# Three gather buffers, spaced weight transfers and another order of places in a mixture-of-experts kernel

## The chip, the cores and the metric

The kernel runs on one core of a Trainium2 chip. The metric is device time in microseconds of one execution: a median of 314.38 us over three runs (313.55 to 315.83). Engines are named as the profile names them: PE multiplies matrices (PEld is its weight load), DVE and ACT work elementwise, POOL does iotas, small elementwise work and the indirect transfers, SP issues the plain transfers. Sixteen DMA engines serve all transfers.

## The reference, cut to what matters

Attention with a causal window of 128 positions and four sink positions is computed for 4 batches of 8 heads, 768 positions and 64 columns. Its rows, 3072 of 512 columns, go into a mixture of 8 experts with a capacity of 80 rows each:

```
logits = x @ w_gate;  expert_idx = argmax(logits);  gate_w = softmax(logits)[expert_idx]
for e in range(8):
    tok_idx = rows with expert_idx == e, the 80 with the largest gate_w if there are more
    h = maximum(x[tok_idx] @ w1[e], 0)
    out[tok_idx] = gate_w[tok_idx] * (h @ w2[e])      # all other rows of out stay 0
```

w1[e] is 512 x 1024 and w2[e] 1024 x 512, both float32: 2 MB each, 33.5 MB for all experts.

## The kernel before, in words

The program has three stages. The attention (up to about 195 us of the profile) works in ticks and writes its rows to the scratch tensor x_rows. The ranking (to about 212 us) finds for each expert the row numbers of its 80 tokens, in idx_in. The experts' stage follows, and the change lies there.

**Experts.** For each expert e, an indirect transfer on POOL gathers its 80 rows into xg_e (line 1210). `tokens(e)` turns them on PE into px (line 1245), which DVE copies to xs. `ffn1(e)` is 128 matmuls with w1 into ph (line 1259), `ffn2(e)` 128 matmuls with w2 into py (line 1274), `rows(e)` turns the result back (pry, line 1290) and scatters it to the output by an indirect transfer on POOL (line 1302). PE's order is written out by hand: ffn1(0), tokens(1), ffn1(1), tokens(2), ffn2(0), ffn1(2), tokens(3), rows(0), ffn2(1), and so on; the last blocks are ffn1(7), rows(5), ffn2(6), ffn2(7) with rows(6) in its middle, rows(7). So there are 16 blocks of 128 matmuls.

**Weights.** A weight matrix comes as two halves of 1 MB, each by four transfers of 256 KB from SP (`load_weight`, lines 288 to 303). The 32 halves are numbered n = 0 to 31 in the order of use; block number j of PE uses n = 2j and 2j + 1. There are 17 places in SBUF (NA + NB + NC = 6 + 7 + 4). Ten halves are issued during the attention and the ranking (n = 0 to 9). Seven more, n = 10 to 16, are issued in the loop of lines 1209 to 1214, where with `hold=True` POOL first writes one element of the place (line 298): the transfer has to wait for that write, and the write stands on POOL behind the gather of the same turn. Half n = 17 + k takes the place of an earlier half, which `in_home` chooses, and waits until PE has read that half for the last time. Before, this is the half number 1 + 7k // 4 (through `in_home`, for a place used twice, the first user's place).

**What sets the order on SP.** Every transfer of SP signals one of eight semaphores, in turn, and waits first until the transfer eight places before it, on the same semaphore, has landed. So at most eight transfers of SP are under way. Up to the weight n = 16 the order of SP is written out (`manual_schedule`); behind that the planner of the library places the transfers where it finds them ready.

Of the kernel before, what the change touches and what calls it, by code (L numbers as in the profile page):

```python
# [8 lines left out]
F32 = mybir.dt.float32  # L9
# [11 lines left out]
E, F = 8, 1024  # L21
DM = H * D
# [5 lines left out]
SINK, WIN, CAP = 4, 128, 80  # L28
# [215 lines left out]
def attention_moe(ctx: ExitStack, tc, q, k, v, n_sink, window, w_gate, w1, w2, capacity, q_t, k_t, v_t, vs_t, wg_t, out):  # L244
    nc = tc.nc
# [37 lines left out]
    wsrc = [(which, e, half) for which, e in order for half in range(2)]  # L283
    wtiles = {}
    homes = [(wpool, n) for n in range(NA)]
    in_home = []

    def load_weight(hold=False):
        n = len(wtiles)
        which, e, half = wsrc[n]  # L290
        src = (w1, w2)[which][e].rearrange("(g c p) f -> g p c f", g=2, p=P)[half]

        k = n - NA - NB - NC
        in_home.append(n if k < 0 else in_home[1 + 7 * k // 4])
        pool, m = homes[in_home[n]]
        t = pool.tile([P, 2 * F], F32, tag=f"w{m}", name=f"w_{which}_{e}_{half}", bufs=1)
        if hold:
            po.memset(t[0:1, 0:1], 0.0)
        to = t.rearrange("p (c f) -> p c f", c=src.shape[1])
        for i in range(0, 2 * F, DM):  # L300
            c, f = divmod(i, src.shape[2])
            nc.sync.dma_start(to[:, c, f:f + DM], src[:, c, f:f + DM])
        wtiles[(which, e, half)] = t

    zeros = const.tile([P, DM], F32, name="zeros")
# [2 lines left out]
    with ExitStack() as actx:  # L308
        wk = actx.enter_context(tc.tile_pool(name="wk", bufs=2))
        sm = actx.enter_context(tc.tile_pool(name="sm", bufs=2))  # L310
# [17 lines left out]
        NG = B * NPB  # L328
# [598 lines left out]
        for n in range(NA):  # L927
            at(W0 + WD * n, load_weight)
# [67 lines left out]
        with tc.manual_schedule():  # L996
            n = 0
# [87 lines left out]
            for _ in range(2):  # L1085
                load_weight()
# [3 lines left out]
            rows_keep_scaled(g0, 1, "xr")  # L1090
            rows_write(g0, 1, nc.sync)
            load_weight()
            gate_logits(i, 1)
            keys_turn(i - 1, 1)
# [68 lines left out]
    with ExitStack() as fctx:  # L1163
# [2 lines left out]
        wk = fctx.enter_context(tc.tile_pool(name="fw", bufs=2))  # L1166
        sm = fctx.enter_context(tc.tile_pool(name="fsm", bufs=1))
        xg = {}
        for e in range(E):
            xg[e] = sm.tile([CAP, DM], F32, name=f"xg_{e}")  # L1170
        chain = ExitStack()
        chain.enter_context(tc.manual_schedule(engines={ve.engine, po.engine}))
        with ExitStack() as sctx:
# [28 lines left out]
        with ExitStack() as wctx:  # L1202
            wps = wctx.enter_context(tc.tile_pool(name="ps_warm", bufs=1, space=PSUM))
            wt = wps.tile([P, 512], F32, name="warm1")
            for _ in range(20):
                pe.matmul(wt[0:CAP, 0:480], hot[:, NNEW - 1], hot[:, 0:6].rearrange("p t c -> p (t c)"), start=True, stop=True)
        line = ExitStack()
        line.enter_context(tc.manual_schedule(engines={nc.sync.engine}))
        for e in range(E):
            po.indirect_dma_start(out=xg[e], out_offset=None, in_=x_rows,  # L1210
                                  in_offset=bass.IndirectOffsetOnAxis(ap=idx_in[:, e:e + 1], axis=0),
                                  bounds_check=NT - 1, oob_is_err=False)
            if e > 0:
                load_weight(hold=True)
        while len(wtiles) < NA + NB + NC:
            load_weight(hold=True)
        line.close()
        gsel = sm.tile([CAP, E], F32, name="gsel")
        po.tensor_tensor(gsel, tab[:, 0], tab[:, 1], ALU.add)
# [22 lines left out]
        def tokens(e):  # L1242
            px = ps_xs.tile([P, DC, CAP], F32, tag="px", name=f"px_{e}")
            for c in range(DC):
                pe.transpose(px[:, c], xg[e][:, c * P:(c + 1) * P], ident[0:CAP, 0:CAP])  # L1245
            xts[e] = wk.tile([P, DC, CAP], F32, tag="xs", name=f"xs_{e}")
            ve.tensor_copy(xts[e], px)  # L1247

        def ffn1(e):
            need(0, e)  # L1250
            x = xts.pop(e)
            h = wk.tile([P, HC, CAP], F32, tag="h", name=f"h_{e}")
            for half in range(2):
                ph = ps_h.tile([P, HC // 2, CAP], F32, tag="ph", name=f"ph_{e}_{half}")
                for f in range(HC // 2):
                    fc = half * (HC // 2) + f
                    for c in range(DC):
                        for m in range(2):
                            pe.matmul(ph[m * D:(m + 1) * D, f], columns(0, e, c, fc * P + m * D),  # L1259
                                      x[:, c], start=(c == 0), stop=(c == DC - 1), skip_group_check=True)  # L1260
                ac.activation(h[:, half * (HC // 2):(half + 1) * (HC // 2)], ph, AF.Relu)  # L1261
            hs[e] = h
# [41 lines left out]

        chain.enter_context(tc.manual_schedule(engines={pe.engine, ac.engine}))
        tokens(0)
        for e in range(E):
            ffn1(e)
            if e + 1 < E:
                need(0, e + 1)  # L1310
                tokens(e + 1)
            if e > 1:
                rows(e - 2)
            if e > 0:
                ffn2(e - 1)
# [66 lines left out]
```

## Time and profile before

| | |
|---|---|
| median of three runs | 314.38 us (313.55 to 315.83) |
| the profiled execution, its own time | 318.28 us |
| its span, first to last instruction | 316.5 us |
| mean granted TensorE clock in it | 0.969 |
| PE busy (matmuls) | 285.1 us, 90% |
| weight transfers of 256 KB | 128, median 5.5 us from issue to landing |

Of the 316.5 us, PE is busy nearly throughout, so the profile is read by stage. From 218.1 us, where ffn1(0) begins, to 310 us PE works on the experts; the windows view gives the share of the 16 DMA engines and the transferred GB/s of each stretch, the chain of waits gives the order of PE's work and the idle time between.

### The profile page before, as it was taken

To read this page: it belongs to the slowest core of one execution; us is meant where nothing else is said; L and a number is where in the kernel's file an instruction comes from. 1 tells how busy PE (TensorE), PEld (TensorE's weight loads), DVE (VectorE), ACT (ScalarE), POOL (GpSimd) and SP (SyncE) were. 2 spreads that over 40 slices of the span, in tenths; PEclk is the share of its full clock that TensorE was granted. 3 is DMA by queue.
4 is the path that set the end of the run, shared out by engine and by line. 5 is a ranking of instruction groups with operands and counts; after the bars stand their busy time and mean duration, and the time that the engine had idled before them with its cause. 6 is when DMAs were issued, how large, how long until landed. Compare 5 with 4: busy or idle time off the path is not lost.

```text
span 316.5 us, 10925 instructions
## 1 busy us (share of the span) xinstructions
PE 285.1 (90%) x4253; PEld 228.3 (72%) x4253; DVE 168.6 (53%) x562; ACT 162.2 (51%) x658; POOL 164.7 (52%) x367
## 2 busy tenths in 40 slices
PE   7498999999998999998999999979878988999991
PEld 2265777877777878785768787647777978989880
DVE  5344887785988788899895969940000000000001
ACT  0656787878777787874678765800111111111210
POOL 4297787848898668885748595558101011011111
PEclk9679999999999999999999999969999999999998
DMA  6999125398851699873135002977999998686601
GB/s 189 338 341 405 44 70 197 132 286 275 282 201 70 227 272 386 352 218 121 42 127 202 34 35 63 304 301 212 278 383 382 372 382 287 207 260 209 248 25 51
DMA packets 32747, 69.71 MB, mean 220 GB/s; under 512 B 4272, under 2 KB 5296, under 8 KB 32304
## 3 DMA queue, kind: packets, MB, share of 16 engines
q1 hardware_dynamic: 31664, 66.31, 61.3%
q0 software_dynamic: 1024, 2.62, 2.9%
q8 instruction: 36, 0.59, 0.8%
q14 instruction: 23, 0.19, 0.2%
HBM read 55.02 MB, written 13.89 MB: 218 GB/s over the span
## 4 chain that ended last, share of the span: by engine, by line
PE 60%; DVE 15%; ACT 9%; issue 7%; POOL 6%; DMA 2%; POOLq 0%; ACTq 0%; DVEq 0%
PE ph L1259 12%; PE sc L510 12%; PE py L1274 12%; PE xp L604 7%; PE pp L563 6%; ACT prob L547 4%; DVE gt L768 3%; ACT pt L575 2%; PE pl L670 2%; DVE gt L765 2%; DVE sc L530 2%; DVE nm L537 2%; PE warm L420 2%; PE pr L637 2%; PE xp L598 1%
## 5 line engine op out<-in xcount | busy, mean ns | idle before, releaser
L547 ACT ACTIVATE prob<-sc,nm 128x132 f32<-128x132 f32 (+1 forms) x192 | 68.9, 377 | 4.6 <-DVE nm L537 4.5
L510 PE MATMUL sc<-k,q 64*128 64x260 f32 (+1 forms) x384 | 58.7, 410 | 8.9 <-ACT prob L547 8.4
L1302 POOL DMA_INDIRECT out_dram<-y,idx x8 | 7.3, 918 | 82.0 <-ACT y L1291 71.9
L575 ACT COPY pt<-pp 128x512 f32<-128x512 f32 x48 | 28.2, 587 | 42.1 <-PE pp L563 34.6
L510 PEld LDWEIGHTS sc<-k,q 64*128 64x128 f32 x384 | 30.8, 190 | 24.4 <-ACT prob L547 15.6
L530 DVE COPY_PREDICATED sc<-upper,sc 128x256 f32<-128x256 int8 x80 | 33.8, 422 | 19.8 <-PE sc L510 11.2
L1259 PE MATMUL ph<-xs,w 128*64 128x80 f32 x1024 | 38.9, 233 | 5.5 <-issue 4.4
L537 DVE TENSOR_REDUCE nm<-sc 128x2 f32<-128x264 f32 (+1 forms) x96 | 41.4, 431 | 3.3
L1247 DVE COPY xs<-px 128x320 f32<-128x320 f32 x8 | 3.9, 492 | 72.7 <-PE px L1245 66.6
L1274 PE MATMUL py<-h,w 128*64 128x80 f32 x1024 | 38.6, 234 | 4.0 <-issue 3.5
L1259 PEld LDWEIGHTS ph<-xs,w 128*64 128x64 f32 x1024 | 37.0, 137 | 6.9 <-issue 5.3
L1274 PEld LDWEIGHTS py<-h,w 128*64 128x64 f32 x1024 | 36.5, 137 | 6.2 <-issue 4.6
L547 ACT ACTIVATION_READ_ACCUMULATOR prob<-sc,nm 128x1 f32 x192 | 40.7, 212 | 0.0
L583 POOL TENSOR_SCALAR_AFFINE_SELECT own<-pt 128x512 f32<-128x512 f32 (+1 forms) x48 | 28.6, 595 | 20.3 <-ACT pt L575 19.6
L604 PE MATMUL xp<-pt,v 128*64 128x128 f32 x384 | 37.4, 288 | 0.0
L563 PEld LDWEIGHTS pp<-ident,prob 128*128 128x128 f32 x192 | 20.8, 144 | 16.5 <-issue 10.5
L563 PE MATMUL pp<-ident,prob 128*128 128x128 f32 x192 | 32.3, 292 | 0.0
L604 PE MATMUL xp<-own,v 128*64 128x128 f32 x320 | 31.1, 273 | 0.0
L590 POOL TENSOR_SCALAR_AFFINE_SELECT pt<-pt 128x512 f32<-128x512 f32 (+1 forms) x48 | 27.8, 578 | 3.3
L1261 ACT ACTIVATE h<-ph 128x320 f32<-128x320 f32 x16 | 7.0, 438 | 43.0 <-PE ph L1259 33.9
L604 PEld LDWEIGHTS xp<-pt,v 128*64 128x64 f32 x384 | 21.4, 137 | 3.5 <-POOL pt L590 0.2
L654 POOL TENSOR_TENSOR xr<-xr,rs 128x512 f32<-128x512 f32 x21 | 22.0, 1049 | 2.9 <-ACT xr L642 2.7
(177 smaller groups left out, 470.7 us busy)
## 6 DMA issues: line engine op xcount, KB each, us to landing
w<-in_moe_w_dram SPq DMA_DIRECT2D x128, 256.0 KB, 5.5
v<-in_v_t_dram SPq DMA_DIRECT2D x12, 512.0 KB, 7.2
out_dram<-zeros SPq DMA_DIRECT2D x24, 256.0 KB, 3.0
x_rows<-xr SPq DMA_DIRECT2D x24, 256.0 KB, 2.5
q<-in_q_t_dram SPq DMA_DIRECT2D x11, 512.0 KB, 7.1
k<-in_k_t_dram SPq DMA_DIRECT2D x3, 1584.0 KB, 8.3
k<-in_k_t_dram SPq DMA_DIRECT2D x1, 1056.0 KB, 9.5
vst_raw<-in_vs_t_dram SPq DMA_DIRECT2D x4, 256.0 KB, 6.8
```

The costliest lines, as they stand in the source:

```text
L510: pe.matmul(sc[:, h, c0:c0 + w], qs[g][r, hp, j % 2 * P:(j % 2 + 1) * P], ks[b][r, hp, k0:k0 + w], start=True, stop=True)
L530: ve.copy_predicated(own, upper, sc[:, :, 0:P])
L537: ve.tensor_reduce(out=nm, in_=sc[:, :, lo_c:hi_c], axis=AX.X, op=ALU.max, negate=True)
L547: ac.activation(prob[:, a, h, p0:], sc[:, h, lo_c:hi_c], AF.Exp, bias=nm[:, h:h + 1], scale=1.0, accum_out=ssum[:, n, 2 * hp + h:2 * hp + ...
L563: pe.transpose(pp[:, a, h], prob[:, a, h, SINK:], ident)
L575: ac.copy(pt, st.pop((t, "pp")))
L583: po.affine_select(out=own[:, a0:], in_=pt[:, a0:], pattern=[[0, 2 - a0], [0, 2], [1, P]], compare_op=ALU.is_ge, fill=0.0, base=0, channel ...
L590: po.affine_select(out=pt[:, a0:], in_=pt[:, a0:], pattern=[[0, 2 - a0], [0, 2], [-1, P]], compare_op=ALU.is_gt, fill=0.0, base=0, channel ...
L604: pe.matmul(xp[h * D:(h + 1) * D, a * P:(a + 1) * P], val[:, (2 * hp + h) * D:(2 * hp + h + 1) * D], pr[:, a, h], start=False, stop=(a == ...
L654: po.tensor_tensor(xr, xr, gst[(i0, "rs")][:, n, :, None].to_broadcast([P, H, D]), ALU.mult)
L1259: pe.matmul(ph[m * D:(m + 1) * D, f], columns(0, e, c, fc * P + m * D), x[:, c], start=(c == 0), stop=(c == DC - 1), skip_group_check=True)
L1274: pe.matmul(to[m * D:(m + 1) * D, dc], columns(1, e, k, dc * P + m * D), h[:, k], start=(k == 0), stop=(k == HC - 1), skip_group_check=True)
```

## The change

It has four parts. (1) Three gather buffers take the place of eight: gathers 0 to 2 are issued at first, gather e + 3 behind `tokens(e)`, into the buffer that `tokens(e)` has read. (2) Of the seven halves n = 10 to 16 only the first two are held by a write of POOL. (3) From n = 10 on, three transfers of one element stand among every five transfers of weights: 88 weight transfers get 52 small ones, from wg_t into the tile `spaced`. (4) Half 17 + k takes the place of half k.

```diff
@@ -284,6 +284,7 @@
     in_home = []
+    spaced = []
 
     def load_weight(hold=False):
@@ -291,7 +292,7 @@
         k = n - NA - NB - NC
-        in_home.append(n if k < 0 else in_home[1 + 7 * k // 4])
+        in_home.append(n if k < 0 else in_home[k])
         pool, m = homes[in_home[n]]
@@ -300,6 +301,11 @@
             c, f = divmod(i, src.shape[2])
             nc.sync.dma_start(to[:, c, f:f + DM], src[:, c, f:f + DM])
+            if spaced:
+                j = spaced[0]
+                if 3 * (j + 1) // 5 > 3 * j // 5:
+                    nc.sync.dma_start(spaced[1][0:1, j:j + 1], wg_t[0:1, 0, 0:1])
+                spaced[0] += 1
         wtiles[(which, e, half)] = t
@@ -1166,8 +1172,8 @@
         xg = {}
-        for e in range(E):
-            xg[e] = sm.tile([CAP, DM], F32, name=f"xg_{e}")
+        NG = 3
+        xgs = [sm.tile([CAP, DM], F32, name=f"xg_{n}") for n in range(NG)]
@@ -1204,16 +1210,22 @@
+        spaced += [0, sm.tile([1, 4 * len(wsrc)], F32, name="spaced")]
         line = ExitStack()
         line.enter_context(tc.manual_schedule(engines={nc.sync.engine}))
-        for e in range(E):
+
+        def gather(e):
+            xg[e] = xgs[e % NG]
             po.indirect_dma_start(out=xg[e], out_offset=None, in_=x_rows,
                                   in_offset=bass.IndirectOffsetOnAxis(ap=idx_in[:, e:e + 1], axis=0),
                                   bounds_check=NT - 1, oob_is_err=False)
+
+        for e in range(NG):
+            gather(e)
             if e > 0:
                 load_weight(hold=True)
         while len(wtiles) < NA + NB + NC:
-            load_weight(hold=True)
+            load_weight()
         line.close()
@@ -1245,6 +1257,8 @@
             ve.tensor_copy(xts[e], px)
+            if e + NG < E:
+                gather(e + NG)
```

**SP, from the last weight of the ranking (n = 9, w_1_1) on.** A name such as w_3_0 gives the expert and the half (the matrix is left out, the last number is the buffer's). Before:

```order
L302 DMA w_1_1_3464<-in_moe_w_dram 128x512 x4
L302 DMA w_3_0_3668<-in_moe_w_dram 128x512 x4
L302 DMA w_3_1_3677<-in_moe_w_dram 128x512 x4
L302 DMA w_2_0_3686<-in_moe_w_dram 128x512 x4
L302 DMA w_2_1_3695<-in_moe_w_dram 128x512 x4
L302 DMA w_4_0_3704<-in_moe_w_dram 128x512 x4
L302 DMA w_4_1_3713<-in_moe_w_dram 128x512 x4
L302 DMA w_3_0_3722<-in_moe_w_dram 128x512 x4
```

The same place now:

```order
L303 DMA w_1_1_3464<-in_moe_w_dram 128x512 x4
L307 DMA spaced<-in_wg_t_dram 1x1 x12
L303 DMA w_3_0_3664<-in_moe_w_dram 128x512 x2
L307 DMA spaced<-in_wg_t_dram 1x1
L303 DMA w_3_0_3664<-in_moe_w_dram 128x512 x2
L307 DMA spaced<-in_wg_t_dram 1x1
L303 DMA w_3_1_3675<-in_moe_w_dram 128x512
L307 DMA spaced<-in_wg_t_dram 1x1
L303 DMA w_3_1_3675<-in_moe_w_dram 128x512 x2
L307 DMA spaced<-in_wg_t_dram 1x1
```

The pattern of two, two and one weight with a small transfer behind each group begins with n = 10, but twelve small transfers stand in front of it.

**SP, behind the part that is written out (from the last transfers of n = 16 on), now:**

```order
L307 DMA spaced<-in_wg_t_dram 1x1
L303 DMA w_3_0_3713<-in_moe_w_dram 128x512
L303 DMA w_3_1_4354<-in_moe_w_dram 128x512 x4
L303 DMA w_5_0_4362<-in_moe_w_dram 128x512 x4
L303 DMA w_5_1_4369<-in_moe_w_dram 128x512 x4
L303 DMA w_4_0_4530<-in_moe_w_dram 128x512 x4
L303 DMA w_4_1_4537<-in_moe_w_dram 128x512 x4
L303 DMA w_6_0_4544<-in_moe_w_dram 128x512
L307 DMA spaced<-in_wg_t_dram 1x1
L303 DMA w_6_0_4544<-in_moe_w_dram 128x512
L307 DMA spaced<-in_wg_t_dram 1x1
```

The twelve small transfers that the code puts among the 20 of n = 17 to 21 are those that the planner has moved to the front: these 20 weight transfers stand without any between them, and from n = 22 on the pattern is back.

**POOL, from its last write of the ranking (parts) on.** Before:

```order
L1140 TENSOR_TENSOR parts<-later,os 128x8
L1210 DMA xg_3589<-x_rows,idx_in 80x512
L1210 DMA xg_3590<-x_rows,idx_in 80x512
L298 MEMSET w_3_0_3668 1x1
L1210 DMA xg_3591<-x_rows,idx_in 80x512
L298 MEMSET w_3_1_3677 1x1
L1210 DMA xg_3592<-x_rows,idx_in 80x512
L298 MEMSET w_2_0_3686 1x1
```

Now:

```order
L1219 DMA xg_3591<-x_rows,idx_in 80x512
L299 MEMSET w_3_1_3675 1x1
L1231 TENSOR_TENSOR gsel<-tab 80x8
L1232 TENSOR_TENSOR gsel<-gsel,tab 80x8
L1219 DMA xg_3589<-x_rows,idx_in 80x512
L1219 DMA xg_3590<-x_rows,idx_in 80x512
L1219 DMA xg_3591<-x_rows,idx_in 80x512
L1219 DMA xg_3589<-x_rows,idx_in 80x512
L1316 DMA out_dram<-y_4052,idx 3072x512
L1219 DMA xg_3590<-x_rows,idx_in 80x512
L1316 DMA out_dram<-y_4208,idx 3072x512
```

Gathers 3 to 6 stand in front of the first scatter and gather 7 between the first two; each waits for PE's px of the buffer's last user.

## Rows read from the trace of the kernel before

**Rows 1.** The page: span and DMA queues (packets, MB, share of 16 engines).

```profile
span 316.5 us, 10925 instructions
...
q1 hardware_dynamic: 31664, 66.31, 61.3%
...
q8 instruction: 36, 0.59, 0.8%
```

**Rows 2.** Who waited for whom from 208 us on: us, times, longest.

```profile
PEld py L1274 <- DMA w<-in_moe_w_dram: 0.7, 1, 0.7
...
PE ph L1259 <- issue: 4.4, 6, 1.0
PE py L1274 <- issue: 3.5, 4, 1.8
```

**Rows 3.** The chain of waits in the experts' stage: start us, us, what.

```profile
231.86 1.76 issue
233.62 3.05 PE py L1274 x82
236.68 0.07 PE ph L1259
...
236.75 1.52 PE ph L1259 x44
238.27 0.73 issue
239.00 3.12 PE ph L1259 x83
...
244.38 0.51 issue
...
267.04 0.55 issue
267.59 4.10 PE py L1274 x113
...
297.64 0.36 PE ph L1259 x4
...
303.72 2.43 PE py L1274 x64
```

**Rows 4.** Windows of 10 us: engines' busy us, then PE clock, DMA share, GB/s.

```profile
230.00:240.00 10.00, 7.51 (x203) 7.13 (x203) 0.49 (x1) 0.60 (x2) 0.00 (x0) 1.00 1.05 385
...
270.00:280.00 10.00, 10.00 (x268) 9.61 (x265) 0.49 (x1) 1.99 (x4) 0.91 (x1) 1.00 0.66 218
```

**Rows 5.** DMA view of the stretch from 236.4 to 236.5 us.

```profile
q8 instruction: 1, 0.02, 68.4%
```

**Rows 6.** DMA view of the stretch from 269.6 to 269.9 us.

```profile
q8 instruction: 1, 0.02, 18.4%
```

**Rows 7.** DMA view of the stretch from 298.8 to 299.1 us.

```profile
q8 instruction: 1, 0.02, 28.4%
```

**Rows 8.** Tile w on SP, from 240 to 258 us (durations in ns: min/median/max).

```profile
L302 SPq DMA_DIRECT2D w<-in_moe_w_dram x26: 327/328/1205, 239.8 to 257.5; - x26
...
DMA to landing us min/median/max: 5.2/5.6/5.9
```

**Rows 9.** Tile w on SP, from 265 to 273.5 us.

```profile
L302 SPq DMA_DIRECT2D w<-in_moe_w_dram x8: 328/430/622, 265.5 to 272.5; - x8
...
DMA to landing us min/median/max: 2.6/3.6/4.9
```

**Rows 10.** SP's own waits, from 214 us on: us, times, longest.

```profile
SPq L302 <- PE ph L1259: 11.2, 4, 4.1
SPq L302 <- PE py L1274: 9.3, 4, 3.6
SPq L302 <- POOL w L298: 6.9, 1, 6.9
```

**Rows 11.** Timeline from 207 to 224 us: start us, us, what.

```profile
208.67 0.21 POOL L1140 TENSOR_TENSOR parts<-later,os 128x8 f32<-128x8 f32 x1
...
214.01 0.96 POOL L1210 DMA_INDIRECT xg<-x_rows,idx_in  x1 [0.31 <-issue]
214.97 0.09 POOL L298 MEMSET w<- 1x1 f32 x1
```

**Rows 12.** Tile xg, whole span.

```profile
DMA to landing us min/median/max: 3.2/8.1/9.2
```

**Rows 13.** Tile ints: a transfer of a few bytes from SP.

```profile
L450 SPq DMA_DIRECT2D ints<-in_window_dram x1: 328/328/328, 10.8 to 10.8; - x1
```

## The prediction

> **What bounds the kernel now.** The change touches only the experts' stage, so I read that stage. First the list of waits: on PE's matmuls of the two blocks the idle time that counts waits for no engine and hardly for a weight (0.7 us once); it is put down to "issue", 4.4 us in 6 pieces and 3.5 us in 4 [rows 2]. That is 7.9 us in ten stalls, and PE is busy through the rest of the stage. Then the chain of waits, for where the stalls stand. Between the one that ends at 233.62 and the next at 238.27 PE does 82 + 1 + 44 = 127 matmuls [rows 3]. The others stand at the same distance, so it is a count of instructions and not a place in the program that makes them. A matmul has a weight load beside it, so 127 pairs are some 255 instructions.
>
> Next the DMA queues: queue 8, named instruction, moves 36 packets of together 0.59 MB, 16.4 KB each [rows 1]. PE's stalls are its own program arriving late, in blocks of some 256 instructions. The views of the single packets give their delay. PE resumes at 233.62 and the next such packet starts between 236.4 and 236.5 [rows 3, 5], 2.8 to 2.9 us later. A packet takes 1.1 us (0.8% of 16 engines times 316.5 us, over 36 [rows 1]), and 1.4 to 1.5 us after its end PE resumes, at 239.00 [rows 3]. I read this as: the next block is asked for when PE enters the one in hand. From asking to use it is then 5.4 us here (239.00 - 233.62), while 127 pairs take 4.65 us (233.62 to 238.27) or, with eight transposes among them, 5.38 us (239.00 to 244.38) [rows 3]. The missing part is the stall.
>
> The delay goes with the number of weights under way. From 240 to 258 us, 26 transfers go out in 17.7 us, one per 0.71 us, each landing after 5.6 us [rows 8]: eight are under way, at 385 GB/s and a DMA share of 1.05 [rows 4]. With four under way [rows 9], PE resumes at 267.59 and the packet starts between 269.6 and 269.9 [rows 3, 6], 2.0 to 2.3 us later. With nearly none, PE resumes at 297.64 and the packet starts between 298.8 and 299.1 [rows 3, 7], 1.2 to 1.5 us later. With 2.55 us for the packet and its arrival, the whole delay is 5.4 us at eight, 4.6 to 4.9 at four, 3.8 to 4.1 at none, against the 4.65 to 5.38 us that a block lasts.
>
> **The change part by part.** *The small transfers* take three of SP's eight semaphores, so that five weights and not eight are under way. The delay with five lies between the row at four and the row at eight: 4.6 to 5.4 us. I take 4.9, nearest to four, which is the mean length of a block: the stalls go, but for 0.5 us in all. The bounds for the eight or so blocks concerned are 0 and 8 times half of 0.55 us [rows 3], 2.2 us.
>
> *Their order* gives some back. Between n = 17 and 21 the 20 weights stand without small ones, so eight are under way again for 20 x 0.71 = 14.2 us. With 28 spaced weights from 215.1 us on, that is about 235 to 249 us, two or three blocks. Stalls under eight are 0.51 to 0.73 us there [rows 3]; I take 2.5 x 0.6 = 1.5 us, bounds 0.5 and 2.2. The twelve small ones in front can go once POOL's last write of the ranking is done, 208.88 us, and the first weight behind them waits anyway for POOL's hold at 214.97 [rows 11], a wait in which SP stood 6.9 us [rows 10]. Twelve issues of 0.33 to 0.43 us [rows 8, 9, 13] and one round of landings fit in; if not, n = 10 comes 1 us late, and PE needs it only in block 5, around 250 us. Cost nothing, under that cover.
>
> *SP's time*: 52 issues more. A small one took 0.33 us [rows 13], weights without a wait 0.43 [rows 9]: five weights with three small ones cost SP at most 8 x 0.43 = 3.44 us, with one long issue of 1.2 us [rows 8] 4.6 us, where five weights need 5 x 0.71 = 3.55 us of DMA. SP can become slower than the DMA engines. What covers that: the last half is wanted by ffn2(7), which starts at 303.72 [rows 3], and the loads end at 215.1 + 88 x 0.71 + 3 = 281 us at the DMA's pace; at SP's worst pace 215.1 + 68/5 x 4.6 + 14.2 + 3 = 295 us. Nothing is late.
>
> *The places*: SP waited 11.2 + 9.3 us for PE to free a place [rows 10], and the DMA share fell to 0.66 there [rows 4]. Half k is free earlier than half 1 + 7k // 4, so these waits go. On PE that is worth nothing, as no weight was late; what it triggers is that the loads crowd into 215 to 281 us. More blocks see a full DMA, none behind it does. Without the spacing that would be more stalls; with it, it is in the 0.5 us above.
>
> *The gathers*: five of 0.96 us on POOL [rows 11] leave the start and follow px. They land after 3.2 to 9.2 us [rows 12], and tokens(e + 3) comes at least two blocks, 10 us, later; this is hidden. On POOL each stands before a scatter that waits for later work of PE anyway. The five holds and five early gathers no longer delay n = 12 to 16, which PE does not wait for. Cost nothing.
>
> **The sum.** 7.9 - 0.5 - 1.5 = 5.9 us off PE's line, which runs on to the last scatter. The profiled execution took 318.28 us (span 316.5) and would take 312.4. The median stands 3.9 us below that execution; the difference is not in these rows, so I take the 5.9 us off the median: 308.5 us. With the bounds, 7.9 - 2.2 - 2.2 = 3.5 to 7.9 - 0.5 = 7.4 us, that is 307.0 to 310.9.
>
> **The rivals.**
>
> *Depth does not matter.* The packet may be late because the engines are busy at all, not because of what is queued. For it: share 1.05 with eight, and I have no row with five. Against it: two packets with busy engines around them, 2.8 us at eight and 2.0 to 2.3 us at four. Then every block from 223 to 281 us stalls, some ten of 0.6 to 0.8 us, about 7 us: 313.5 us, 0.9 less than now. [...]
>
> *Half of it.* Five under way behave nearer to eight, and a stall of some 0.3 us stays at each block: 7.9 - 10 x 0.3 - 1.5 = 3.4 us, 311.0. The spread of the delays at four allows it.
>
> *Slower: five under way do not fill the DMA.* If each weight still needs its 5.6 us [rows 8] with five under way, five take 5.6 us instead of 3.55. The last half is then there at 215.1 + 68/5 x 5.6 + 14.2 + 3 = 308.5 us, where ffn2(7) would start at 303.72 - 5.9 = 297.8: 10.7 us of waiting for 5.9 won, 319.2 us. It decides where the round takes over 5.25 us; at 4.9 the loads are in time but for 1 us. For it: the slowest of the rows at four took 4.9 us [rows 9]. Against it: others there took 2.6, and the 5.6 us are 8 x 0.71, a queue and not a latency.
>
> **How the numbers follow.** The forecast has 0.60, half of it 0.15, depth without effect 0.15, slower 0.10. The predicted time is the forecast's 308.5. The range of 306.5 to 313.7 takes in its bounds, the half and most of the case without effect, and leaves about 0.2 out, mostly on the slow side. A measurement of this kernel tells 1%, 3.1 us, from no change. Faster by over 1% (under 311.2): 0.60 and most of the half, 0.69. Within 1%: the case without effect, the rest of the half and the mild end of the slow case, 0.24. Slower by over 1%: 0.07.
>
> **What would show it.** In the chain of waits after, "issue" pieces on PE between 223 and 300 us should sum to about 2 us and stand mostly between 235 and 255. Landing of weights should be near 3.5 us outside that stretch and 5.6 in it. The last weight should be issued before 285 us and the DMA stand empty after. SP should no longer wait for PE. It would be wrong if "issue" pieces stay at 0.5 us and more with landings of 3.5 us (depth does not matter), or if PE waits for DMA w from about 285 us on (loads too slow).

## The result, and the profile after

Over 20 runs each the changed kernel has a median of 312.88 us (308.21 to 317.28), the kernel before 316.13 us (312.08 to 318.75): ratio 0.9886, interval 0.9854 to 0.9917. The ratio leaves out the executions that lie over 1.5% above their kernel's fastest. By it the change is worth 3.6 us (the two medians differ by 3.25), where 5.9 of 314.38 us (ratio 0.981) were forecast. In a later session the same two gave 0.979 (0.972 to 0.986). The direction held, and so did the cure of the stalls; the wait for late weights, which the sum put at nothing, was several us.

The profiled execution took 313.70 us. First its page and the list of waits from 214 to 300 us (engine, line and tile that waited, what for; us, times, longest), which answer to [rows 1, 2, 10]:

```profile
span 312.0 us, 10964 instructions
...
q1 hardware_dynamic: 31768, 66.31, 63.3%
...
q8 instruction: 36, 0.59, 0.8%
```

```profile
PEld py L1288 <- SPq L1342: 2.7, 3, 2.0
...
PE py L1288 <- SPq L1342: 2.2, 3, 1.8
PE ph L1273 <- issue: 2.0, 2, 1.6
...
PEld py L1288 <- DMA w<-in_moe_w_dram: 0.2, 1, 0.2
```

The instruction packets are as many as before. "Issue" on PE's matmuls fell from 7.9 to 2.0 us and is absent from the blocks of py; a wait that was not there has come, on py, for "SPq L1342". The list of SP's own waits no longer has PE's 20.5 us:

```profile
SPq L303 <- DMA w<-in_moe_w_dram: 26.6, 48, 1.8
...
SPq L303 <- PE ph L1273: 0.3, 1, 0.3
```

The timeline of PE shows where both stand (start us, us, line, tiles, count, in brackets the idle time before it and what ended it). First 249 to 256 us, then the last two blocks:

```profile
249.78 2.31 PE L1288 MATMUL py<-h,w 128*64 128x80 f32 x61
251.86 1.13 PE L1273 MATMUL ph<-xs,w 128*64 128x80 f32 x26
254.58 1.61 PE L1273 MATMUL ph<-xs,w 128*64 128x80 f32 x41 [1.59 <-issue]
```

```profile
289.34 4.96 PE L1288 MATMUL py<-h,w 128*64 128x80 f32 x128
294.88 0.91 PE L1288 MATMUL py<-h,w 128*64 128x80 f32 x20 [0.58 <-ACT yt L1296]
297.61 0.36 PE L1288 MATMUL py<-h,w 128*64 128x80 f32 x4 [1.81 <-SPq L1342]
298.14 0.42 PE L1288 MATMUL py<-h,w 128*64 128x80 f32 x4 [0.17 <-SPq L1342]
298.77 2.67 PE L1288 MATMUL py<-h,w 128*64 128x80 f32 x36 [0.21 <-SPq L1342]
301.37 0.78 PE L1304 MATMUL pry<-ident,yt 128*80 128x128 f32 x4
302.08 2.43 PE L1288 MATMUL py<-h,w 128*64 128x80 f32 x64
```

The 1.59 us stand where eight weights are under way again, n = 17 to 21 (issued from 239.7 to 254.7 us), as the prediction had it. That these are the cause is not shown: the kernel with six in order, below, stalls longest at the same place. The other wait is in the first half of ffn2(7). The releaser's name there, an instruction of SP's queue at the program's end, is a guess of the view. The counts tell more: the first 32 matmuls of this half go through the eight blocks of rows of w2 in turn, four matmuls each, and each of the last four blocks is one transfer of n = 31. PE does 20, then stops, does four, four, and then the rest: it stood before the last three transfers. SP issued the last at 293.50 us. The windows view (busy us of each engine, PE's clock, DMA share, GB/s), to be held against [rows 4]:

```profile
230.00:240.00 10.00, 10.00 (x272) 9.72 (x270) 0.49 (x1) 1.98 (x4) 1.91 (x2) 1.00 0.95 293
270.00:280.00 10.00, 10.00 (x276) 9.72 (x271) 0.49 (x1) 2.12 (x5) 0.91 (x1) 1.00 0.89 300
...
295.00:302.00 7.00, 4.80 (x68) 3.95 (x68) 0.00 (x0) 0.00 (x0) 0.00 (x0) 0.76 0.23 77
```

PE is busy in the whole of both old windows. The DMA engines move 293 and 300 GB/s in these two windows, where before it was 385 and then 218. In the last window the granted clock is 0.76, after PE had stood: 1.00 up to 298 us, 0.50 from 299 to 301 us (over the same window it is 1.00 in the one profile of this kernel without such a wait, the last below). Of ffn2(7)'s first half 36 matmuls took 2.67 us, where 64 take 2.43. So the late weights cost more than the 2.2 us of waiting: this half took 7.20 us (294.88 to 302.08). Before it took 2.92, from the first of these lines to the second:

```profile
303.72 2.43 PE L1274 MATMUL py<-h,w 128*64 128x80 f32 x64 [0.58 <-ACT yt L1282]
...
306.64 2.44 PE L1274 MATMUL py<-h,w 128*64 128x80 f32 x64
```

### The profile page after: what moved, and what is told of

Its sections match the earlier page's. It is cut to its first block, busy times and chain, and to the rows that moved or that the text cites. A ratio compares the mean times of both kernels' runs of the same rounds, so it can differ in the third digit from the quotient of the medians.

```text
span 312.0 us, 10964 instructions
## 1 busy us (share of the span) xinstructions
PE 283.7 (91%) x4253; PEld 228.3 (73%) x4253; DVE 168.3 (54%) x562; ACT 161.9 (52%) x658; POOL 164.4 (53%) x362
## 5 line engine op out<-in xcount | busy, mean ns | idle before, releaser
L516 PE MATMUL sc<-k,q 64*128 64x260 f32 (+1 forms) x384 | 57.9, 405 | 9.1 <-ACT prob L553 8.7
L1288 PE MATMUL py<-h,w 128*64 128x80 f32 x1024 | 39.8, 238 | 2.9 <-SPq L1342 2.2
L1288 PEld LDWEIGHTS py<-h,w 128*64 128x64 f32 x1024 | 37.4, 140 | 5.3 <-SPq L1342 2.7
L1273 PE MATMUL ph<-xs,w 128*64 128x80 f32 x1024 | 37.9, 233 | 3.3 <-issue 2.0
L569 PEld LDWEIGHTS pp<-ident,prob 128*128 128x128 f32 x192 | 20.5, 143 | 16.2 <-issue 10.1
L1219 POOL DMA_INDIRECT xg<-x_rows,idx_in x8 | 8.0, 996 | 31.2 <-PE px L1257 25.9
```

The source lines that it names most:

```text
L516: pe.matmul(sc[:, h, c0:c0 + w], qs[g][r, hp, j % 2 * P:(j % 2 + 1) * P], ks[b][r, hp, k0:k0 + w], start=True, stop=True)
L569: pe.transpose(pp[:, a, h], prob[:, a, h, SINK:], ident)
L1288: pe.matmul(to[m * D:(m + 1) * D, dc], columns(1, e, k, dc * P + m * D), h[:, k], start=(k == 0), stop=(k == HC - 1), skip_group_check=True)
```

## Experiments

Sixteen runs were made, in four sessions on three chips, some of them of a kernel that had run already; each ratio is against the kernel before in the same session. "Stage" is from the first matmul of ffn1(0) to the first of ffn2(7) in the profile, "half" from there to ffn2(7)'s second half, "issue" that of PE's matmuls in the experts' stage, the transposes among them. Each profile is one execution.

| kernel | ratio (95%) | stage, half us | issue us | last weight issued |
|---|---|---|---|---|
| before, three profiles | 1 | 85.6, 85.1, 84.4; 2.9 | 7.9, 6.1, 7.0 | 294.2, 292.4, 292.8 |
| changed, three profiles | 0.9886 (0.985 to 0.992); 0.979 (0.972 to 0.986) | 78.6, 78.8, 77.3; 7.2, 2.9, 6.7 | 2.0, 2.2, 1.6 | 293.5, 292.7, 291.9 |
| no small transfers (8) | 1.008 (1.004 to 1.012) | 83.1; 2.9 | 5.6 | 283.8 |
| seven in order | 0.997 (0.992 to 1.001) | 83.4; 2.9 | 5.5 | 284.7 |
| six in order, twice | 0.989 (0.983 to 0.996); 0.978 (0.972 to 0.985) | 78.8, 80.2; 2.9 | 2.9, 2.6 | 290.2, 288.6 |
| five in order | 1.003 (0.999 to 1.006) | 81.0; 6.5 | 0 | 296.3 |
| five, last 24 free | 0.989 (0.984 to 0.994) | 79.3; 3.6 | 0.2 | 292.5 |
| transfers of 128 KB, none small | 1.121 (1.116 to 1.127) | 121.3; 7.9 | 1.1 | 340.0 |

**How many are under way.** The small transfers were left out, or put in a fixed order on SP (so that the twelve no longer run ahead), in three proportions:

```diff
# no small transfers
-        spaced += [0, sm.tile([1, 4 * len(wsrc)], F32, name="spaced")]
# in order: SP's written order to the end of the stage
-        line = ExitStack()
-        line.enter_context(tc.manual_schedule(engines={nc.sync.engine}))
+        chain.enter_context(tc.manual_schedule(engines={nc.sync.engine}))
...
-        line.close()
# six; seven
-                if 3 * (j + 1) // 5 > 3 * j // 5:
+                if 2 * (j + 1) // 6 > 2 * j // 6:
+                if (j + 1) // 7 > j // 7:
```

> The changed kernel without its small transfers: gathers and places as changed, eight weights under way throughout. Theory A (the queue of weights delays PE's instruction blocks; five under way cure it, and the price is that the loads get slower and the last weights come late): the stalls are back, some ten blocks of 0.6 to 0.7 us, 6 to 7 us in all, and the late weights at the end (4.4 us) are gone: about 2 us above the changed kernel, ratio to the kernel before 0.992 to 1.000, issue pieces of 6 us and more from 218 us on. Theory B (the stalls went for another reason, the order of places or the gathers): few stalls, no late weights, ratio to before about 0.975.

> The changed kernel with SP's order written out to the end, so that the small transfers stand where the program has them: five weights under way throughout, also for the 20 weights that had none between them. Theory A: the stall of 1.6 us of the stretch 241 to 252 us goes, but 20 weights take 0.95 us each instead of 0.7, the last weight comes 4 to 5 us later, and PE waits for it: 4 to 5 us above the changed kernel, ratio to before 1.000 to 1.007, PE's wait inside ffn2(7) 8 to 11 us instead of 4.4. Theory C (the wait at the end comes from the twelve small transfers in front or from a single late transfer, not from the pace of the loads): no later than the changed kernel, ratio 0.98 to 0.99.

> As the kernel in order, but two small transfers per six weights: six under way throughout. Theory A: a weight takes about 0.8 us, the loads end at about 213 + 88 x 0.8 = 284 us and nothing is late; stalls small, 0.2 us in ten blocks: 4 us below the changed kernel, ratio to before 0.973 to 0.982. Theory D (five is needed, six stalls like eight): stalls of 0.5 us and more at most blocks, ratio 0.99 to 1.00.

> As the kernel in order, but one small transfer per seven weights: seven under way. Theory A: a weight takes 0.73 us, nothing is late, stalls of about 0.4 us at ten blocks, 3 to 4 us: ratio to before 0.98 to 0.99, between six and eight under way. Theory D: as with eight, 0.99 to 1.00.

Issue is 5.6, 5.5, 2.9 and 2.6, 0 us for eight, seven, six, five. Theories B and D fall, though seven stalls as eight does, where I had expected 3 to 4 us and a ratio of 0.98 to 0.99. That no block stalls with five in order, while every one has as many instructions as before, shows that the depth of the loads delays PE's program: in the traces of the kernel before and of the changed one each of the twelve stalls ends 2.3 to 3.2 us behind the start of a packet of queue 8, named instruction. The series does not part the bytes that are queued from the rate at which they move: from 260 to 280 us that falls too, 370, 358, 323 and 285 GB/s. Against the rival by which the number queued does not matter as long as the engines are busy stands the DMA share in the same stretch: 1.02 with eight, where issue is 5.6 us, and still 0.89 with five, where it is 0.

Another queue may play a part. The kernel with six in order has its longest stall at 254.83 us, with never more than six weights under way, and the changed kernel has one of 1.56 to 1.59 us there in each of three profiles:

```profile
254.83 2.37 PE L1271 MATMUL ph<-xs,w 128*64 128x80 f32 x63 [1.82 <-issue]
```

From 250 to 256 us a gather and a scatter moved together here, in queue 0. The DMA view of that stretch, for six in order and then for the kernel before, which has none of queue 0:

```profile
q1 hardware_dynamic: 868, 1.58, 78.1%
q0 software_dynamic: 128, 0.33, 15.1%
```

```profile
q1 hardware_dynamic: 1271, 2.31, 103.8%
q8 instruction: 1, 0.02, 1.2%
```

The three profiles of the changed kernel have 127 or 128 of these packets there. But with 121 of them five in order has no stall there, and with 128 the second profile of six in order has one of 0.35 us. So they are a candidate for the long stall, not its shown cause.

The loads pay for the smaller depth. The view of the tile w on SP from 255 to 280 us gives the transfers issued in those 25 us and the time from issue to landing, for eight, seven, six and five under way:

```profile
L303 SPq DMA_DIRECT2D w<-in_moe_w_dram x33: 327/328/1248, 255.0 to 279.4; - x33
...
DMA to landing us min/median/max: 4.9/6.2/7.0
```

```profile
L303 SPq DMA_DIRECT2D w<-in_moe_w_dram x32: 327/328/1227, 255.2 to 279.5; - x32
...
DMA to landing us min/median/max: 4.4/5.1/6.7
```

```profile
L303 SPq DMA_DIRECT2D w<-in_moe_w_dram x30: 327/328/1079, 255.1 to 279.7; - x30
...
DMA to landing us min/median/max: 3.9/4.9/6.5
```

```profile
L303 SPq DMA_DIRECT2D w<-in_moe_w_dram x26: 327/328/1417, 255.6 to 279.2; - x26
...
DMA to landing us min/median/max: 3.1/4.6/6.4
```

From seven to five a transfer lands hardly sooner, 5.1 to 4.6 us, so fewer under way means fewer landed: one per 0.76, 0.78, 0.85 and 0.94 us. Five in order issues its last weight at 296.3 us. PE waits for weights from 278 us on, sooner than expected, and for less inside ffn2(7) (the half takes 6.5 us):

```profile
PE ph L1271 <- DMA w<-in_moe_w_dram: 2.3, 2, 1.4
PE py L1286 <- DMA w<-in_moe_w_dram: 1.6, 3, 0.8
```

Theory A holds, theory C falls. Besides seven, two sizes of mine were off: without small transfers the kernel is slower than expected (1.008, not 0.992 to 1.000), though its one profile, 316.0 us of a median of 318.0, shows no reason; and six gained less than expected in the first of its two comparisons.

**The end alone.** Five in order, with no small transfers among the last 24 weights:

```diff
-            if spaced:
+            if spaced and n < 26:
```

> Five under way, in order, for the first 64 weights from half 10 on, and no small transfers for the last 24. If the late weights of the kernel with five throughout (last issue 296.3 us) were the pace of the loads: 24 weights at 0.7 instead of 0.94 us put the last issue at about 290.5 us, nothing is late, and the price is a stall of 0.5 to 1 us at two or three of the last blocks: below five in order by 1% or more, ratio to before 0.980 to 0.992 by the chip. If the late weights have another cause, as five in order, within 0.5% of the kernel before.

As expected in the time, 1.4% below five in order (across two sessions), and the late weights became fewer but did not go: the last is issued at 292.5 us, not 290.5, and PE waits 2.9 us for weights from 284 us on. The stalls that I expected in the last blocks, with eight under way again, did not come (0.2 us of issue); the waits for weights there may have given PE's program the time, which no run shows.

**Bytes or transfers.** Without small transfers, every weight transfer from n = 10 on cut in two of 64 rows:

```diff
-            nc.sync.dma_start(to[:, c, f:f + DM], src[:, c, f:f + DM])
+            for p in (range(0, P, P // 2) if n >= NA + 4 else (0,)):
+                q = P // 2 if n >= NA + 4 else P
+                nc.sync.dma_start(to[p:p + q, c, f:f + DM], src[p:p + q, c, f:f + DM])
```

> No small transfers; from half 10 on each weight transfer is cut in two of 64 rows, 128 KB: eight are under way as in the kernel without small transfers, but with half the bytes. If the bytes queued ahead of PE's instruction packet make the stalls: issue on PE falls from 5.6 us to 2 us or less, as with four of 256 KB; the loads are slower than with five, 1.0 us or more per 256 KB, and the end waits for them: ratio 1.00 to 1.02. If it is the number of transfers under way: stalls of 5 us and more, as without small transfers.

```profile
PE py L1289 <- DMA w<-in_moe_w_dram: 18.6, 20, 2.1
PE ph L1274 <- DMA w<-in_moe_w_dram: 9.2, 6, 2.1
...
PE py L1289 <- issue: 1.1, 4, 0.4
```

Issue is nearly gone, but this does not tell bytes from transfers, because fewer than eight were under way. SP's own waits from 214 to 340 us show it, here first and then for whole transfers without small ones:

```profile
SPq L305 <- POOL w L299: 6.2, 1, 6.2
SPq L305 <- PE ph L1274: 0.8, 1, 0.8
```

```profile
SPq L303 <- DMA w<-in_moe_w_dram: 27.1, 59, 1.7
```

By this view SP never waited for the transfer eight places before. An issue took 595 ns (median; 328 for a whole transfer), close to the 0.70 us between two issues, so SP set the pace. The loads fell to 202 GB/s from 260 to 280 us, far worse than expected. Whether bytes or transfers count stays open.

**Each part on the kernel before.**

```diff
# small transfers only, in order: the edits on load_weight, spaced and SP's order alone
# places only
-        in_home.append(n if k < 0 else in_home[1 + 7 * k // 4])
+        in_home.append(n if k < 0 else in_home[k])
# gathers only: the edits on xg, gather(e) and the holds alone
# six in order, eight gathers
-        NG = 3
+        NG = 8
```

> The kernel before with three small transfers to five weights (in order, five under way), its eight early gathers and its old places. Theory A (five under way cures the stalls, and makes the loads slow): the 7.8 us of issue on PE fall to 2 us or less, and the last weights come late, since SP also still waits for places: PE waits inside the last three blocks for 3 to 7 us, ratio to before 0.99 to 1.005. If the small transfers were not the cause of the shorter stalls, issue stays at 6 us and more.

> The kernel before with only the places changed (half 17 + k takes the place of half k). Theory F (the later gathers made the kernel without small transfers 0.8% slower; the places do nothing): ratio 0.995 to 1.003, SP's 20 us of waiting for PE gone, stalls about as before, 7 to 8 us. Theory G (the places do the harm, since the loads crowd into fewer blocks): ratio 1.005 to 1.012 with 9 us of stalls or more.

> The kernel before with only the gathers changed: three at first, one more behind each of the first five token blocks, three buffers, two holds. Theory F: the packets of a gather stand ahead of PE's instructions in the stretch from 222 to 265 us, the stalls grow by 0.3 to 0.6 us at five blocks: ratio 1.004 to 1.010, issue pieces of 1.5 us and more where queue 0 moved packets just before the instruction packet. Theory G (a gather is hidden, as the prediction had it): 0.998 to 1.003.

> Six under way in order and the new places, but all eight gathers at first, as in the kernel before, with their seven holds. Theory F: the one long stall of the kernel with six (1.8 us at 253 to 255 us, behind 101 packets of queue 0) goes, and 1 to 3 us with it: ratio to before 0.980 to 0.986. Theory G: as with six and three gathers, 0.987 to 0.992. Were the early gathers worth something themselves, over 0.993.

Measured: small transfers alone 1.001 (0.998 to 1.004), places alone 1.006 (1.002 to 1.010), gathers alone 0.996 (0.993 to 1.000), six with eight early gathers 0.991 (0.987 to 0.994). Small transfers alone cut issue to 3.2 us, all of it in ffn1(0): no later block stalls, though gathers and places are the old ones, which bears out the cure by depth. The last half takes 5.0 us, so the late weights are there too. (This profile, 312.6 us, is the fastest of twelve executions with a median of 317.2.) The prices of theory F did not come; its mechanism is not refuted. With the gathers alone issue is 8.1 us, with pieces of 2.4 and 1.8 us, and with six and eight early gathers the stall near 254 us is 0.3 us instead of 1.8, but ffn1(0) stalls for 3.0. The times fit theory G, but its mechanism isn't shown: issue in the kernel with the places alone is 8.0 us, about as in the kernel before (7.9, 6.1, 7.0), and 3.0 of that stand in a place that I had not expected. Its first block is slow:

```profile
216.25 2.04 PE L1259 MATMUL ph<-xs,w 128*64 128x80 f32 x45 [0.58 <-issue]
219.37 0.37 PE L1259 MATMUL ph<-xs,w 128*64 128x80 f32 x3 [1.07 <-issue]
220.78 0.33 PE L1259 MATMUL ph<-xs,w 128*64 128x80 f32 x3 [1.05 <-issue]
221.51 0.23 PE L1259 MATMUL ph<-xs,w 128*64 128x80 f32 x1 [0.40 <-issue]
222.24 4.51 PE L1259 MATMUL ph<-xs,w 128*64 128x80 f32 x76 [0.50 <-issue]
```

128 matmuls took 10.5 us instead of 4.65; from 222 to 227 us the granted clock was 0.66. The other two kernels here with eight early gathers show the same (8.7 and 10.3 us), none with three.

**Does the kernel before have that block too?** It was profiled twice more, and the changed kernel too:

> The kernel before, profiled once more. If its first block is as in the profile shown (ffn1(0) in 4.65 us, ten stalls of together 7.8 us), the 8.7 to 10.5 us that ffn1(0) took in three kernels with eight early gathers come from what those kernels changed. If ffn1(0) takes 8 us and more here too, the early gathers cost the kernel before 4 to 6 us in some of its executions, which the profile shown did not contain, and part of the gain is that.

> The same once more, since the first block may differ between executions: ffn1(0) in 4.65 us in both, or over 8 us in at least one of them.

> The changed kernel, profiled a third time: ffn1(0) in 4.65 us and 1 to 3 us of issue as in the two others; the wait for the last weights was 4.3 us in one and absent in the other. If it is a matter of where a few slow transfers fall, it lies between 0 and 4.5 us here; if the pace of the loads sets it, the last weight is issued after 292 us, with the first half of ffn2(7) over 2.93 us wherever PE comes to it before 295 us.

In both further profiles of the kernel before ffn1(0) takes 4.65 us, so nothing in three profiles says that the gain of the change is this. What makes the block slow in the three others stays open. The changed kernel shows the late weights in this profile too, 6.65 us for the half, after reaching ffn2(7) at 293.5 us.

**Once more side by side, and five buffers** (six in order, `NG = 5`):

> The changed kernel once more, to stand beside the next one on the same chip: ratio to before 0.985 to 0.992 and, in its trace, 1 to 3 us of issue on PE and 3 to 5 us of waiting for the last weights inside ffn2(7).

> Six under way in order, once more beside the changed kernel. If the wait for the last weights is what the changed kernel lacks to its forecast, it is 2 to 4 us below it: ratio to before 0.976 to 0.984, and ffn2(7) runs its first half in 2.9 us. If that wait is worth nothing over many executions, both stand at 0.989.

> Six under way in order with five gather buffers: five gathers at first, three later. The kernels with eight early gathers showed, in three profiles of four, matmuls coming by threes and fours for 4 us in ffn1(0), and hardly any stall later; those with three none of the first, and one stall of 1.8 us near 254 us. If the count of early gathers sets both: the slow stretch in ffn1(0) is short or absent, the stall near 254 us is under 0.6 us, ratio 0.5 to 1% below the kernel with six and three buffers. If five are already too many: the slow stretch is there, and the ratio is that of six with eight early gathers, 0.991.

In one session the changed kernel gave 0.979, six 0.978, six with five buffers 0.982 (0.977 to 0.987): no difference that can be told, where I had expected each to be ahead of the one before it. In this profile of the changed kernel the last transfers came in time, by little, against my expectation of 3 to 5 us of waiting:

```profile
290.12 4.72 PE L1288 MATMUL py<-h,w 128*64 128x80 f32 x128
295.41 2.44 PE L1288 MATMUL py<-h,w 128*64 128x80 f32 x64 [0.57 <-ACT yt L1296]
```

PE reached ffn2(7) 0.5 us later than in the first profile, the last weight was issued 0.8 us earlier. So the late weights are a race at the edge, lost in two profiles of three. Six wins it in both its profiles and keeps 0.8 us more of stalls; by the profiles it should be ahead by 1.4 us, which the times don't show. With five buffers ffn1(0) took 5.8 us, between 4.65 and the 8.7 to 10.5 of eight. No version beat the changed kernel.

## Why the prediction was right in kind and wrong in size

**Stalls of PE's program: right, its place in part by luck.** 2.0 us were to be left, mostly between 235 and 255 us; it was 2.0, 2.2 and 1.6 us, the largest piece ending at 254 to 256 us each time. The prediction put the rest down to two or three blocks of 0.6 us under eight weights; most of it is one stall of 1.6 us, which six under way have as well. The stage shrank by 6.8 us (means of three profiles: 85.0 to 78.2): 5.1 us of issue (7.0 to 1.9; the 7.9 of the prediction are the highest of three), some 0.6 us of waiting for a weight that two profiles of before have, and 1.1 us that I can't assign. The rival by which depth doesn't matter is out, and "half of it" as a mechanism too.

**The pace of the loads: the step that failed.** "Nothing is late" put the wait for the last weights at nothing. It rested on five weights needing 3.55 to 4.6 us, so that SP's worst case still ended at 295 us, and on landings of 3.5 us. Its own sign of being wrong came, PE waiting for weights behind 285 us, and the last weight was issued not before 285 us but at 291.9 to 293.5. In the changed kernel 27 transfers were issued from 254.7 to 279.8 us:

```profile
L303 SPq DMA_DIRECT2D w<-in_moe_w_dram x27: 327/328/1182, 254.7 to 279.8; - x27
```

That is 0.97 us each, 4.8 us per five. The landings in the changed kernel are not in its views; with five in order, at nearly the same pace, they took 4.6 us. My 3.5 us came from bursts of four that found the engines emptying (DMA share 0.72 from 265 to 270 us, 0.58 from there to 273.5) [rows 9]; in a steady stream I have no landing that short in the median. The rival "slower" had the mechanism: with 4.83 us its formula gives 215.1 + 68/5 x 4.83 + 14.2 + 3 = 298.0 us for the last weight, and PE went on with it at 298.77. That the two are so close is partly luck, as the first weight went out at 213.3 us and the twenty without small ones took 16 us instead of 14.2. By that formula PE waits as soon as a round takes over 4.8 us; the 5.25 us that I gave is where the wait eats the whole gain, and with "a queue and not a latency" I dismissed the case. In addition PE reached ffn2(7) not at 297.8 but at 293.5 to 295.4 us: in the first profile 1.8 us of that is an earlier start of ffn1(0) and 1.2 a greater gain in the stage. The price of the late weights is 4.3, 0 and 3.7 us in three profiles, 2.7 in the mean: 6.8 - 2.7 = 4.1 us, against 3.6 measured in one comparison and 6.7 (0.021 of 318.5) in the other. Why the sessions differ by so much is open; the changed kernel's median was nearly the same in both (312.88, 313.25 us), that of the kernel before was not (316.13, 318.54).

**The places and gathers: costed at nothing, and not nothing alone.** With eight under way the places cost 0.6% and the gathers gain 0.4%, each hardly clear of its interval. SP's waits for PE did go, as predicted. With the old places, the early gathers and five under way the kernel is where it was (1.001); its profile loses 4.0 us in ffn1(0) and 2.1 by late weights. Which of places and gathers the change needs beside the small transfers, no run tells. The later gathers are not free of a suspicion either: they bring the packets of queue 0 to 250 us.

## What to carry to other kernels

Stalls at a fixed count of instructions were here the sign of a program that arrived late: ten of 0.47 to 1.76 us, some 127 matmuls or a multiple of that apart, each behind a packet of queue 8. Fewer transfers under way cured them: 2.0 us were left of 7.9, and none with five in order. Before one throttles a stream so, one divides the transfers under way by the landing time of a full stream, not of a burst (here 4.6 us with five in order, 3.6 us in the burst of four), and compares the resulting end with when the consumer comes after its gain. A saving upstream moves the deadline of every transfer behind it: rivals are to be worked out with the new times.

## What the runs showed that was not expected

- The landing time of 256 KB falls less than the depth: 6.2, 5.1, 4.9, 4.6 us at eight, seven, six, five under way (medians of one profile each), where five eighths of 6.2 are 3.9.
- The first matmul of ffn1(0) came between 215.7 and 218.6 us, in kernels of either kind. Between the two first profiles the offset of 1.8 us is there by 34 us, in code that is the same in both (the first matmul of the gate logits at 32.2 and 34.0 us). In the third profile of the changed kernel that matmul comes at 33.7 us, and ffn1(0) begins at 216.2 all the same. In the mean of three profiles each, the changed kernel begins 1.5 us earlier; since kernels with the same gathers begin as late as 217.9 and 218.6, I don't count it to the change. The granted clock from 10 to 20 us was 0.50 to 0.53 in the three profiles of the kernel before and 0.55 to 0.66 in those of the changed one. By the single us it was 0.50 throughout in the first profile of the kernel before, and in that of the changed kernel 0.50 from 12 to 18 us and 0.79 to 1.00 in the rest.
- In three kernels a block of matmuls came by threes for 4 us (above). In two of them the clock fell behind it: it was 0.66 from 222 to 227 us with the places alone, 0.59 from 224 to 228 us with six and eight early gathers. With the small transfers alone 78 matmuls took 2.97 us from 222.27 us on, the pace of 64 in 2.43 us.
